# First layer in seven block products: batches 4 to 7 and all tails of a forgetting attention with a two-layer network, on one core

## The chip, the cores and the metric

The kernel runs on one core of one Trainium2 chip. The metric is the device time of one execution in microseconds (us); runs of the kernel before took 1084.06, 1081.60 and 1083.31, median 1083.31.

A core has five engines with instruction queues of their own, each worked through strictly in order: TensorE (PE, matmuls into eight PSUM banks), VectorE (DVE), ScalarE (ACT), GpSimd (POOL) and SyncE (SP), which here only issues DMA transfers.

## The reference

```python
# attention: B, H, S, D = 8, 8, 576, 64
scores = scale * np.matmul(q, k.transpose(0, 1, 3, 2))
cum = np.cumsum(np.log(np.clip(f, 0.0001, 1.0)), axis=-1)
decay = cum[:, :, :, None] - cum[:, :, None, :]
scores = np.where(causal, -1000000000.0, scores + decay)
attn = np.exp(scores - np.max(scores, axis=-1, keepdims=True))
attn = attn / (np.sum(attn, axis=-1, keepdims=True) + 1e-09)
attn_out = np.matmul(attn, v)
# network: 4608 tokens, 512 -> 2048 -> 512
x = attn_out.transpose(0, 2, 1, 3).reshape(B * S, H * D)
h = x @ w_in
g = np.maximum(h, 0.0) + alpha * np.minimum(h, 0.0)
out = g @ w_out
```

All inputs are 32-bit floats (the two weights come as 64-bit floats and are converted on the chip). To keep precision, a product of the network is made of three matmuls: each factor is split into a rounded part (hi) and the rest (lo), and hi x hi, hi x lo and lo x hi are added up in PSUM.

## The kernel before, in words

**Attention** goes over 32 head pairs n (8 batches of 4 pairs). For a pair, `load_n` fetches q, k and the decay rows and splits q and k into hi and lo (ScalarE copies, GpSimd subtracts; the first NN = 4 pairs use plain 32-bit matmuls instead and no split). `attention` then makes scores in stretches of TensorE, masks them and takes row minima on VectorE, takes exponentials on ScalarE, transposes on TensorE, evacuates on ScalarE, multiplies by v and divides by the sums, which go through a small DRAM tile `rd` to become rows. A batch has 576 tokens; the network takes the first 512 of each batch as one column group, and the last 64 of all eight batches together as a ninth group of 512, the *tails* (batch number 8 in the code, collected in the DRAM tile `xt`). `rest` divides, splits x into hi and lo and leaves it in the ring `rx` (seven buffers, four per batch).

**First layer**, `ffn1(b)`: for each of 16 blocks `fc` of 128 hidden features, 12 matmuls of 512 columns into one bank, in two halves of six; then ScalarE and VectorE apply the slopes and the result goes to the DRAM tile `hd`. For the groups in `LATE` = (0, 7, 8) the slopes are applied only later, in the second layer. The first weight is converted from 64 bits in `load_w_in`/`split64` (VectorE bit operations, ScalarE copies, GpSimd subtraction) during the early pairs.

**Second layer**, `ffn2(u)`, over 18 units of 256 tokens in the order `UNITS`: already in seven block products (the Strassen-Winograd scheme, `PRODS`): per unit 8 x 21 matmuls of 256 columns. Its factors are sums of blocks of h (VectorE), split on ScalarE and VectorE. The second weight is converted and its block sums are made in `load_w_out`, after attention, while the first layer of the last groups runs.

**Order.** Nothing is issued when it is written: `op(engine, ns, fn, key, deps, bufs)` records an operation with an estimated duration, and `Plan.run` is a list scheduler that writes the five queues: at each step the engine's operation that can start earliest, and among those the lowest key. Attention has keys of 10 per pair, the first layer 1e6 and more, so the first layer fills what attention leaves free on TensorE. `Ring` and `Store` hand out buffers in the order of their creation; an operation that needs a buffer waits until one is free. An operation marked `two=True` is planned to wait for GpSimd. At the end of attention `change` closes the pool of attention's buffers and opens those of the second layer (`o_change`, which depends on `done_a`).

Of the kernel before, what the change touches and what calls it, by code (L numbers as in the profile page):

```python
# [8 lines left out]
F32 = mybir.dt.float32  # L9
# [18 lines left out]
NV2 = 6  # L28
NS = 10
HURRY = 25  # L30
CONV0, CONV = 30, 2.2
NW = NF // 2
GW = 2
LATE = (0, B - 1, B)

UNITS = (2, 3, 0, 4, 5, 1, 6, 7, 14, 8, 9, 15, 10, 11, 16, 12, 17, 13)
# [42 lines left out]
SLACK = {"DVE": 1.12, "ACT": 1.08, "POOL": 1.05}  # L79
ENGS = ("PE", "ACT", "DVE", "POOL", "SP", "-")  # L80


class Plan:
# [30 lines left out]
    def run(self):  # L114
# [7 lines left out]
        while left:  # L122
            best = None
            for e in ENGS:
                t0 = self.now[e]
                pick = None
                for o in cand[e]:
# [17 lines left out]
                    if pick is None or (s, o.key) < pick[:2]:  # L145
                        pick = (s, o.key, o)
# [39 lines left out]
def attention_moe(  # L186
# [24 lines left out]
    xt = dram.tile([NP, 128, 512], F32, name="xt")  # L211
# [7 lines left out]
    am = const.tile([128, NF], F32, name="am")  # L219
# [14 lines left out]
    rH, rO = Ring(banks, 2, 4), Ring(banks, 0, 6)  # L234
# [9 lines left out]
    rrq = ring(sp, 2, [128, QW], F32, "rq")  # L244
    rrk = ring(sp, 2, [128, S], F32, "rk")
# [12 lines left out]
    rwa = ring(sp, 1, [128, 512], U32, "wa")  # L258
# [7 lines left out]
    wbf = sp.tile([128, 512], BF16, name="wbf")  # L266
# [29 lines left out]
    def split64(tiles, src, whi, wlo, key, deps, bufs_out):  # L296

        br, ba = Buf(rwr), Buf(rwa)
# [3 lines left out]
        a = lambda: shape(ba.t)  # L302
# [8 lines left out]
        def bits2():  # L311
# [7 lines left out]
                   key, [cp], [ba] + bufs_out) for h in (slice(0, 2), slice(2, 4))]  # L319
# [59 lines left out]
    o_wbf = op("DVE", 300, lambda: ve.memset(wbf, 1.0), -102)  # L379
    bw = Buf(rS)  # L380
    for i in range(7):
        op("PE", 800, lambda: [pe.matmul(bw.t, wbf[:, 0:128], wbf, start=True, stop=True) for _ in range(3)], -200, [o_wbf], [bw])  # L382
# [30 lines left out]
    x_ops, x_late, xt_ops, s_0 = {}, [], [], []  # L413

    def load_n(n, held):
# [4 lines left out]
        bq, bk, bZ = Buf(rrq), Buf(rrk), Buf(rZ)  # L420
        kq = -99 if first else -59 if n == 1 else kl
        dq = [] if first else [o_scan]
        l_q = op("SP", 450, lambda: sy.dma_start(bq.t, qq[b, p]), kq, dq, [bq], kb=320)
        l_k = op("SP", 450, lambda: sy.dma_start(bk.t, kk[b, p]), kq, dq, [bk], kb=288)
# [29 lines left out]
        rt = op("POOL", 260, lambda: po.tensor_tensor(Zt()[:, 512:576], Zt()[:, 512:576], tri2, ALU.add), kc + 0.3, tz + [o_mask], [bZ])  # L454
        if n < NN:
            held += [bq, bk]
            return [l_q, l_k], rz, rt, bZ, [(lambda: bq.t, lambda: bk.t)]
        bQ = Buf(rQ)
        Qh, Ql, Kh, Kl = ((lambda j=j: bQ.t[j]) for j in range(4))
        out = []  # L460
        for hi, lo, raw, ld, w in ((Qh, Ql, bq, l_q, QW), (Kh, Kl, bk, l_k, S)):
            o1 = op("ACT", c_acs(w), lambda hi=hi, raw=raw: ac.activation(hi(), raw.t, AF.Copy), kc, [ld], [raw, bQ])  # L462
            o2 = op("POOL", c_po(w), lambda hi=hi, lo=lo, raw=raw: po.tensor_tensor(lo(), raw.t, hi().bitcast(F32), ALU.subtract), kc, [o1], [raw, bQ])  # L463
            out += [o1, o2]
        held.append(bQ)
# [4 lines left out]
    def attention(n):  # L470
# [28 lines left out]
        def evac(bank, w, key, deps, dst, src, bufs):  # L499
            key -= hurry  # L500
            if b == 0 and w % 256 == 0:
                return op("DVE", c_dve(w), lambda: ve.tensor_copy(dst(), src()), key, deps, [bank] + bufs)  # L502
            return op("ACT", c_act(w), lambda: ac.activation(dst(), src(), AF.Copy), key, deps, [bank] + bufs)  # L503
# [78 lines left out]
        def fetch(key, st_, d):  # L582
            for o, (c0, c1), s0 in ((0, (0, S), 0), (64, (512, S), S), (64, (0, 512), S + 64)):
                ri_ops.append(op("SP", 350, lambda o=o, c0=c0, c1=c1, s0=s0: sy.dma_start(
                    bri.t[o : o + 64, c0:c1], d[s0 : s0 + c1 - c0].rearrange("(o s) -> o s", o=1).broadcast_to([64, c1 - c0])),
                    key, [st_], [bri], kb=(c1 - c0) / 4))

# [93 lines left out]
        def rest():  # L681
            bx, xo = Buf(rx), []
            for r in range(2):
# [3 lines left out]
                late = ri_ops if n < NN else [op("-", 2000, lambda: None, st, ri_ops)]  # L687
                mu = op("DVE", c_dve(w_), lambda r=r, t0=t0, w_=w_: ve.tensor_tensor(bxs[r].t, bxs[r].t, bri.t[:, t0 : t0 + w_], ALU.mult),  # L688
                        st, xs_ops[r] + late, [bxs[r], bri])
                xh = op("ACT", c_acs(256), lambda r=r, t0=t0: ac.activation(  # L690
                    bx.t[:, 0, t0 : t0 + 256], bxs[r].t[:, 0:256], AF.Copy), st, [mu], [bxs[r], bx])
                xl = op("POOL", c_po(256), lambda r=r, t0=t0: po.tensor_tensor(  # L692
                    bx.t[:, 1, t0 : t0 + 256], bxs[r].t[:, 0:256], bx.t[:, 0, t0 : t0 + 256].bitcast(F32), ALU.subtract), st, [xh], [bxs[r], bx])
                xo += [xh, xl]
                x_late.extend((mu, xh, xl))
            xt_ops.append(op("SP", 400, lambda: sy.dma_start(xt[p, :, 64 * b : 64 * b + 64], bxs[1].t[:, 256:320]), k0 + 11.6, [mu], [bxs[1]], kb=32))
            x_late.append(xt_ops[-1])
            x_ops[b, p] = [bx] + xo
# [13 lines left out]
        def values():  # L712
            bP = [Buf(rH if n < NP else rS) for _ in range(2)]
# [25 lines left out]
    w_ready = {}  # L739
    w_in_v = w_in.rearrange("(c p) f -> p c f", p=128)  # L740

    def load_w_in(fc):
        fs = slice(128 * fc, 128 * fc + 128)
        w_ready[fc] = split64(NC4, w_in_v[:, :, fs], lambda: wi[:, fc, 0], lambda: wi[:, fc, 1], CONV0 + CONV * fc, [s_0[6]], [])

    hd_ops, h_pe = {}, {}

    def ffn1(b):

        for fc in range(NF):  # L750
            bh, bs = Buf(rH), Buf(rhs)
            last = None
# [14 lines left out]
            else:  # L767
# [4 lines left out]
            hd_ops[b, fc] = op("SP", 400, lambda bs=bs, fc=fc: sy.dma_start(  # L772
                hd[fc % NW, fc // NW, :, 512 * b : 512 * b + 512], bs.t), -1000, [cp], [bs], kb=256)

# [6 lines left out]
    for fc in range(NF):  # L781
        load_w_in(fc)
    done_a = [o for o in plan.ops if o not in set(x_late)]

    TU = 256  # L790
    later = []

    def ring_later(n, shape, dt, name):
        r = Ring(Store([]))
        later.append((r, n, shape, dt, name))
        return r

    rwo = ring_later(2, [128, DM], U64, "wr2_")
    rwx = Ring(Store([]))
    rhr = ring_later(2, [128, GW, 2, TU], F32, "hr")  # L800
    rgx = ring_later(2, [128, 4, GW, 128], F32, "gx")
    rgh = ring_later(1, [128, 2, 7, GW, 128], F32R, "gh")
    ros = Ring(Store([]))
# [4 lines left out]
    wot = [None] * (NW - NV) + [wid[:, WN * i : WN * i + WN].rearrange("p (k j n) -> p k j n", k=2, j=7) for i in range(NV)]  # L808

    def change():  # L810
        ctx_a.close()
        p1 = ctx.enter_context(tc.tile_pool(name="p1", bufs=1, reuse_waits="tile"))
        for r, n, shape, dt, name in later:
            r.store.items += [p1.tile(shape, dt, name=f"{name}{i}") for i in range(n)]
            r.store.free += [(plan.t, i) for i in range(n)]
        wx.append(p1.tile([128, 2, 8, 256], F32, name="wx"))
        rwx.store.items += [wx[0][:, i] for i in range(2)]
        rwx.store.free += [(plan.t, i) for i in range(2)]
        for i in range(NW - NV):
            wot[i] = p1.tile([128, 2, 7, 256], F32R, name=f"wot{i}")  # L820
# [3 lines left out]
    def change3():  # L824
        st = rhr.store
        for i in range(4):
# [248 lines left out]
```

## Time and profile before

| | |
|---|---|
| median of the runs | 1083.31 us |
| the profiled execution | 1082.03 us |
| its span, first to last instruction | 1080.2 us |
| TensorE busy | 1068.2 us, 99% |
| VectorE, ScalarE, GpSimd busy | 707.3, 699.5, 279.4 us |
| granted TensorE clock, mean | 0.997 |
| HBM read and written | 120.68 and 48.52 MB |

A row of the timeline has the start in us, the length in us, engine, line, operation, output<-inputs (the program's names, buffer numbers left out), shape, and how many instructions were merged; in brackets the idle time before it and what ended it. A row of the groups has the total busy us and the mean ns of one. Matmuls overlap in a pipeline, so the length of a merged row divided by its count is nearer to what one costs than the mean. A row of the windows gives the stretch, its length, and for each engine the busy time and the number of instructions, then the granted clock, the share of the DMA engines and GB/s. Line L322 is the helper that issues most matmuls: `xx,wi` is the first layer, `wot` or `wi` with 256 columns the second, `Kh,Qh` the scores of a pair.

### The profile page before, as it was taken

Reading aid. Unit: us, or ns where it says so; the run is one execution under the profiler, and the core shown is the slowest. Engines: PE = TensorE matmul, PEld = TensorE weight load, DVE = VectorE, ACT = ScalarE, POOL = GpSimd, SP = SyncE. Lnnn points to the kernel's source line nnn. Section 1 sums busy time; section 2 is a strip of 40 time slices with the busy share of each in tenths; the row PEclk is TensorE's granted clock in tenths of the full one; section 3 lists DMA queues with packets and bytes.
Section 4 is the critical chain, followed back from the end, with each engine's and each line's share of the span. In section 5 each row is a group of like instructions: output and inputs, shape, how many; then the busy total and the mean of one; then the engine's idle time right before and its main releaser. Section 6 shows DMA issues by size and latency. Waiting matters only on the chain.

```text
span 1080.2 us, 20892 instructions
## 1 busy us (share of the span) xinstructions
PE 1068.2 (99%) x7428; PEld 910.8 (84%) x7428; DVE 707.3 (65%) x1632; ACT 699.5 (65%) x1638; POOL 279.4 (26%) x407
## 2 busy tenths in 40 slices
PE   8899999999999999999999999999999999999998
PEld 4577777777777777777787888899999999999998
DVE  6896745434434434434433497879989898989994
ACT  6898888967857857857846376656454554646551
POOL 6596774542443433433401000000000000000000
PEclk9999999999999999999999999999999999999999
DMA  6877766663653663553531566563433533443511
GB/s 184 252 221 239 241 193 180 191 182 115 184 174 118 179 181 115 177 177 115 151 104 71 166 221 233 193 206 117 150 126 118 157 118 120 139 134 125 147 61 39
DMA packets 116337, 170.57 MB, mean 158 GB/s; under 512 B 16626, under 2 KB 62601, under 8 KB 116233
## 3 DMA queue, kind: packets, MB, share of 16 engines
q1 hardware_dynamic: 115945, 169.05, 50.2%
q8 instruction: 58, 0.95, 0.4%
q14 instruction: 46, 0.38, 0.1%
q10 hardware_dynamic: 288, 0.20, 0.1%
HBM read 120.68 MB, written 48.52 MB: 157 GB/s over the span
## 4 chain that ended last, share of the span: by engine, by line
PE 96%; DVE 1%; DMA 1%; ACT 0%; POOL 0%; issue 0%; DVEq 0%
PE bank L322 87%; PE bank L507 8%; DMA wr<-in_w_in_dram 1%; PE bank L382 1%; DMA Zt<-c 0%; PE bank L646 0%; PE bank L571 0%; DVE xs L688 0%; ACT es L494 0%; DVE wa L313 0%; POOL Z L437 0%; DVE wa L312 0%; DVE e L527 0%; DVE eT L502 0%; DVE es L624 0%
## 5 line engine op out<-in xcount | busy, mean ns | idle before, releaser
L322 PE MATMUL bank<-xx,wi 128*128 128x512 f32 x1728 | 421.3, 396 | 0.3 <-DVE st L624 0.3
L322 PEld LDWEIGHTS bank<-xx,wi 128*128 128x128 f32 x1728 | 316.7, 188 | 63.3 <-issue 1.9
L770 DVE SCALAR_TENSOR_TENSOR hs<-bank,sa,hs 128x512 f32<-128x512 f32 x96 | 72.0, 750 | 156.6 <-ACT hs L768 156.6
L503 ACT ACTIVATE eT<-bank 128x384 f32<-128x384 f32 x240 | 109.2, 487 | 27.1 <-PE bank L507 23.7
L322 PE MATMUL bank<-wot,xx 128*128 128x256 f32 x1008 | 123.9, 284 | 0.0
L322 PE MATMUL bank<-wi,xx 128*128 128x256 f32 x1008 | 123.9, 284 | 0.0
L322 PEld LDWEIGHTS bank<-wi,xx 128*128 128x128 f32 x1008 | 122.3, 192 | 0.0
L322 PEld LDWEIGHTS bank<-wot,xx 128*128 128x128 f32 x1008 | 122.3, 192 | 0.0
L768 ACT ACTIVATE hs<-bank,ab 128x512 f32<-128x512 f32 x96 | 66.0, 687 | 81.0 <-PE bank L322 78.1
L494 ACT ACTIVATE e<-e,st 128x512 f32<-128x512 f32 (+2 forms) x160 | 109.1, 686 | 5.3 <-DVE st L527 3.4
L322 PE MATMUL bank<-eT,vr 128*64 128x320 f32 (+4 forms) x896 | 94.1, 360 | 0.0
L322 PEld LDWEIGHTS bank<-eT,vr 128*64 128x64 f32 x896 | 57.3, 137 | 40.8 <-issue 7.7
L507 PE MATMUL bank<-ident,e 128*128 128x128 f32 x576 | 87.9, 281 | 3.2 <-DVE st L624 1.6
L507 PEld LDWEIGHTS bank<-ident,e 128*128 128x128 f32 x576 | 68.2, 143 | 22.6 <-ACT e L494 6.0
L692 POOL TENSOR_TENSOR xx<-xs,xx 128x256 fp32r<-128x256 f32 x64 | 49.2, 785 | 146.7 <-ACT xx L690 146.7
L463 POOL TENSOR_TENSOR Ql<-rq,Qh 128x640 fp32r<-128x640 f32 x28 | 44.6, 1592 | 142.6 <-ACT Qh L462 57.8
L964 ACT ACTIVATE xx<-gx 128x1024 fp32r<-128x1024 f32 x48 | 50.8, 1058 | 30.8 <-PE bank L322 15.1
L437 POOL TENSOR_TENSOR Z<-Z,tri 128x384 f32<-128x384 f32 x64 | 61.9, 977 | 16.3 <-DMA Z<-c 8.8
L967 DVE TENSOR_TENSOR xx<-gx,xx 128x1024 fp32r<-128x1024 f32 x48 | 58.6, 1221 | 7.8 <-ACT xx L964 7.8
L322 PE MATMUL bank<-wi,gh 128*128 128x256 f32 x504 | 62.4, 284 | 0.0
L322 PE MATMUL bank<-wot,gh 128*128 128x256 f32 x504 | 62.4, 284 | 0.0
L322 PEld LDWEIGHTS bank<-wot,gh 128*128 128x128 f32 x504 | 61.4, 192 | 0.1
(137 smaller groups left out, 1690.0 us busy)
## 6 DMA issues: line engine op xcount, KB each, us to landing
hd<-hs SPq DMA_DIRECT2D x144, 256.0 KB, 2.0
wx<-hd SPq DMA_DIRECT2D x47, 512.0 KB, 4.1
Z<-c SPq DMA_DIRECT2D x62, 256.0 KB, 4.8
hr<-hd SPq DMA_DIRECT2D x25, 512.0 KB, 3.8
rq<-in_qq_dram SPq DMA_DIRECT2D x32, 320.0 KB, 5.3
vr<-in_vv_dram SPq DMA_DIRECT2D x32, 320.0 KB, 2.9
rk<-in_kk_dram SPq DMA_DIRECT2D x32, 288.0 KB, 3.4
Zt<-c SPq DMA_DIRECT2D x62, 144.0 KB, 5.0
```

The lines of the kernel that those rows point to most:

```text
L322: pe.matmul(o, lhsT, rhs, start=start, stop=stop)
L382: op("PE", 800, lambda: [pe.matmul(bw.t, wbf[:, 0:128], wbf, start=True, stop=True) for _ in range(3)], -200, [o_wbf], [bw])
L437: m1 = op("POOL", c_po(128 * 3), lambda z4=z4: po.tensor_tensor(z4()[:, 6:9], z4()[:, 0:3], tb(3), ALU.add), kc + 0.1, got + [o_mask], [bZ])
L463: o2 = op("POOL", c_po(w), lambda hi=hi, lo=lo, raw=raw: po.tensor_tensor(lo(), raw.t, hi().bitcast(F32), ALU.subtract), kc, [o1], [raw, bQ])
L494: ex = op("ACT", c_exp(w), lambda: ac.activation(bt.t[:, :w], bt.t[:, :w], AF.Exp, bias=lo()[:, col : col + 1], scale=-1.0, accum_out=su() ...
L503: return op("ACT", c_act(w), lambda: ac.activation(dst(), src(), AF.Copy), key, deps, [bank] + bufs)
L507: pe.transpose(t[:, c : c + 128], src[:, 128 * j : 128 * j + 128], ident)
L692: xl = op("POOL", c_po(256), lambda r=r, t0=t0: po.tensor_tensor(bx.t[:, 1, t0 : t0 + 256], bxs[r].t[:, 0:256], bx.t[:, 0, t0 : t0 + 256]. ...
L768: cp = op("ACT", c_act(512), lambda bh=bh, bs=bs, fc=fc: ac.activation(bs.t, bh.t, AF.Relu, scale=ab[:, fc : fc + 1]), -1000, [last, o_sg] ...
L770: cp = op("DVE", c_dve(512), lambda bh=bh, bs=bs, fc=fc: ve.scalar_tensor_tensor(bs.t, bh.t, sa[:, fc : fc + 1], bs.t, ALU.mult, ALU.add), ...
L964: his.append(op("ACT", c_acs(128 * GW * (j1 - j0)), lambda j0=j0, j1=j1, src=src, o_=o_: ac.activation(o_(0, j0, j1), src(), AF.Copy), key ...
L967: rdy.append(op("DVE", c_dve(128 * GW * (j1 - j0)), lambda j0=j0, j1=j1, src=src, o_=o_: ve.tensor_tensor(o_(1, j0, j1), src(), o_(0, j0, ...
```

## The change

1. **Groups of the first layer.** Batches 0 to 3 (`G = 4`) keep the plain `ffn1`. Batches 4 and 5, then the tails, then batches 6 and 7 are done by the new `strassen`: over eight pairs of feature blocks, seven products of six matmuls each (512 columns wide; 256 for the tails). `x_prep` loads x from DRAM, makes four sums and splits seven factors; each factor has one buffer. Results are added on VectorE, get their slopes on ScalarE, a last addition on GpSimd, and go to `hd`.
2. **Pace.** Block fc of batch b may begin only after the first scores of pair `int(PACE(b, fc))`, which rises from 6 to 31; blocks 6 to 15 of batch 3 wait for the last scores of all.
3. **x through DRAM.** Only batch 0 splits x where it is made. All others store it to `xd`; batches 1 to 3 are loaded back and split by `load_x` (ScalarE, GpSimd), 4 to 7 and the tails by `x_prep`.
4. **First weight.** `load_w_in` takes two blocks at a time in the one buffer of `rbx`, makes four block sums on GpSimd and stores them (`wsd`); after attention `load_ws` loads and splits them.
5. **Second weight.** `load_w_out` is spread over pairs 15 to 29 (key 150 + 20c), its block sums are made on GpSimd and stored (`wxd`); `load_wot` loads and splits them while the last group runs, into the space that this group gives up (`HOME`).
6. **Buffers and the planner.** Raw q and k: one buffer of `rraw` (the first pairs alternate with `rbx`) instead of two each. `LATE` is empty, `NV2` is 10 instead of 6, `UNITS` is in another order, products with v have a ring `rP` of their own, and of batch 0 only evacuations of 512 columns stay on VectorE. `Plan.run` sorts by key and, for GpSimd (`YIELD`), takes no operation that would keep one of a lower key waiting by more than 0.5 us.

```diff
-NV2 = 6
+NV2 = 10
-CONV0, CONV = 30, 2.2
+CONV0, CONV = 30, 3
+WO0, WO = 150, 20
+G = 4
+FK = 6
+TAILS = (B - G) // 2 - 1
+P0, P1 = 6, 31
+def PACE(b, fc):
+    return P0 + (P1 - P0) * (NF * b + fc) / (NF * G - NF + FK)
-LATE = (0, B - 1, B)
-UNITS = (2, 3, 0, 4, 5, 1, 6, 7, 14, 8, 9, 15, 10, 11, 16, 12, 17, 13)
+LATE = ()
+UNITS = tuple(range(14)) + (16, 14, 17, 15)
...
-    rrq = ring(sp, 2, [128, QW], F32, "rq")
-    rrk = ring(sp, 2, [128, S], F32, "rk")
-    rwa = ring(sp, 1, [128, 512], U32, "wa")
+    rraw = ring(sp, 1, [128, QW + S], F32, "raw")
+    rbx = ring(sp, 1, [128, 8, 256], F32, "bx")
...
+        def sums():
+            A11, A12, A21, A22, S1, S2, S3, S4 = (bx.t[:, i] for i in range(8))
+            po.tensor_tensor(S1, A21, A22, ALU.add)
+            po.tensor_tensor(S2, S1, A11, ALU.subtract)
+            po.tensor_tensor(S3, A11, A21, ALU.subtract)
+            po.tensor_tensor(S4, A12, S2, ALU.subtract)
+        su = op("POOL", 4 * c_po(256), sums, key + CONV, parts, [bx])
+        ws_ops[pr] = op("SP", 400, lambda: sy.dma_start(wsd[pr], bx.t[:, 4:8]), key + CONV, [su], [bx], kb=512)
...
         for fc in range(NF):
             bh, bs = Buf(rH), Buf(rhs)
-            last = None
+            late = b == G - 1 and fc >= FK
+            n = min(B * NP - 1, int(PACE(b, fc)))
+            last = s_0[-1] if late else s_0[3 * n if n < NE else 3 * NE + 2 * (n - NE)]
...
+    S_PRODS = (0, 1, 5, 4, 6, 2, 3)
+    def strassen(g, n, cols, units, xs_):
+        bX, ready = xs_
+        for pr in range(NW):
...
+            def product(m, dk, W=W):
+                jw, b_, bx = S_PRODS[m], Buf(rH), bX[m]
+                def f_():
+                    for c in range(2):
+                        for i, (k, l) in enumerate(((0, 0), (0, 1), (1, 0))):
+                            mm(b_.t[:, 0:n], W(jw, k, c), bx.t[:, l, c, 0:n], c + i == 0, c == 1 and i == 2)
...
+    o_x8 = op("-", 0, change2, 0, [o for q in xs_[1].values() for o in q])
+    op("-", 0, lambda: add(rgh, [as_gh(wide["xr"][:, 2048 : 2048 + WN])]), 0, [last[1], last[2]])
+    op("-", 0, change3, 0, list(last.values()) + res_ops[GL])
+    HOME = (4, 0, 5, 1, 6, 2, 7, 3)
```

417 lines of the change are left out of this document (283 added, 134 removed).

## The prediction

> **What bounds the kernel now.** I read the page's busy times first, then the chain that ended last, then TensorE's own row in time, stage by stage.
>
> ```profile
> PE 1068.2 (99%) x7428; PEld 910.8 (84%) x7428; DVE 707.3 (65%) x1632; ACT 699.5 (65%) x1638; POOL 279.4 (26%) x407
> PE 96%; DVE 1%; DMA 1%; ACT 0%; POOL 0%; issue 0%; DVEq 0%
> ```
>
> TensorE is busy 99% of the span and carries 96% of the chain, so time falls only with its work or its 12 us of idleness. What one matmul costs cannot be read from the mean durations, since neighbours overlap; it comes from long unbroken rows: start, length, count.
>
> ```profile
> 593.54 120.02 PE L322 MATMUL bank<-xx,wi 128*128 128x512 f32 x528
> 713.39 5.20 PE L322 MATMUL bank<-wot,gh 128*128 128x256 f32 x42
> 718.43 5.20 PE L322 MATMUL bank<-wot,xx 128*128 128x256 f32 x42
> 1066.18 10.24 PE L322 MATMUL bank<-wi,xx 128*128 128x256 f32 x84
> ```
>
> From 593.54 to 713.39 run 528 first-layer matmuls of 512 columns: 0.2270 us each. A second-layer run of 42 with 256 columns takes 718.43 - 713.39 = 5.04 us: 0.1200 each. The second layer goes from 713.39 to 1066.18 + 84 x 0.12 = 1076.3, that is 362.9 us without a gap, and 3.9 us of additions and stores end the span of 1080.2. Of the 1728 first-layer matmuls (9 batches x 16 blocks x 12), 1200 lie before 593.54, inside attention, where they fill what attention leaves free.
>
> ```profile
> 56.06 0.33 PE L322 MATMUL bank<-Kh,Qh 64*128 64x128 f32 x2
> 88.09 0.33 PE L322 MATMUL bank<-Kh,Qh 64*128 64x128 f32 x2
> 56.06:68.49 12.43, 1.66 (x6) 1.00 0.88 255
> 68.49:88.09 19.60, 10.98 (x42) 1.00 0.64 186
> 56.06:68.49 12.43, 11.39 (x92) 8.97 (x91) 12.24 (x36) 10.45 (x32) 10.74 (x12) 1.00 0.88 255
> ```
>
> The first two rows are the first scores of head pairs n=4 and n=6. The next two are windows with the first-layer matmuls alone (window, length, busy, count): 48 of them, 10.9 us, ran before pair 6. The last has all engines (TensorE, weight loads, VectorE, ScalarE, GpSimd): of 12.43 us of pair 4, TensorE was busy 11.39. From 88.09 to 593.54 are 505.5 us with 1152 first-layer matmuls (261.5 us); the other 244 us are the attention of 26 pairs, 9.4 us each.
>
> **The work that goes.** 1728 matmuls of 512 columns become 768 plain ones (batches 0 to 3), 2 x 8 x 7 x 6 = 672 in block products, and 336 of 256 columns for the tails: 288 x 0.2270 = 65.4 us go, 336 x 0.1200 = 40.3 come, net -25.1 us, all of it on TensorE and so on the path.
>
> **The paced stage.** The plain blocks now wait for attention: block k of 54 may start after the first scores of pair 6 + 25k/54, 2.16 blocks (5.9 us) per pair; the other ten wait for the last scores. If TensorE stays full a pair takes 9.4 + 5.9 = 15.3 us. The old kernel already has such pairs:
>
> ```profile
> 344.72:359.36 14.64, 14.64 (x109) 11.36 (x109) 6.41 (x24) 11.96 (x36) 6.31 (x9) 1.00 0.63 186
> 359.36:373.90 14.54, 14.54 (x108) 11.28 (x107) 8.09 (x25) 12.73 (x36) 8.06 (x11) 1.00 0.66 181
> 346.54 1.64 PE L322 MATMUL bank<-xx,wi 128*128 128x512 f32 x6
> 349.36 2.92 PE L322 MATMUL bank<-xx,wi 128*128 128x512 f32 x12
> 357.47 1.63 PE L322 MATMUL bank<-xx,wi 128*128 128x512 f32 x6
> ```
>
> Two whole pairs of 14.64 and 14.54 us with a full TensorE; the first holds 6 + 12 + 6 = 24 first-layer matmuls, two blocks. So 2.16 blocks are about what a pair can swallow, and the old surplus filling is not needed once pairs 8 and later run. Into pairs 15 to 29 comes the conversion of the second weight:
>
> ```profile
> L312 DVE SCALAR_TENSOR_TENSOR wa<-wr,wa 128x512 uint32<-128x512 uint32 x16 | 14.3, 897 | 0.5
> L882 DVE SCALAR_TENSOR_TENSOR wx<-wr,wx 128x512 uint32<-128x512 uint32 x16 | 11.1, 693 | 0.5
> L878 ACT ACTIVATE wx<-wr 128x512 f32<-128x512 f32 x16 | 10.6, 664 | 0.0
> L891 ACT ACTIVATE wx<-wx,sg 128x512 f32<-128x512 f32 x16 | 11.5, 719 | 3.2 <-DVE wx L886 3.2
> L692 POOL TENSOR_TENSOR xx<-xs,xx 128x256 fp32r<-128x256 f32 x64 | 49.2, 785 | 146.7 <-ACT xx L690 146.7
> L690 ACT ACTIVATE xx<-xs 128x256 fp32r<-128x256 f32 x64 | 24.6, 409 | 7.2 <-DVE xs L688 5.8 <-PE bank L322 1.3
> ```
>
> Sixteen halves over 14 pairs are 1.14 a pair: ScalarE 1.14 x (0.664 + 0.719) = 1.6 us, VectorE at most 1.14 x 4 x 0.9 = 4.1 us, GpSimd eight sets of four sums, 8 x 4 x 0.785 / 14 = 1.8 us. Out of pairs 4 and later go two ScalarE copies (0.8) and two GpSimd subtractions (1.6); batches 1 to 3 get them back as reloads, about a quarter. ScalarE thus stands at some 13 to 13.7 of 15.3 us, VectorE at 10 to 12. I take 1 us for all pairs together; the upper bound is the rival below. About 100 DMA issues are added to SyncE's in-order queue in attention (w_out loads, x stores and reloads, two kinds of weight stores) and some 46 stores of the first layer leave it; a store that waits for GpSimd's sums holds back the loads behind it, and those of q and k now have one raw buffer.
>
> Row and rule here: the same instruction took 897 ns in the first weight's conversion, beside a busy GpSimd, and 693 ns in the second's, beside an idle one. [...]
>
> **The start.** Pairs 4 and 5 now run with no filling, and the raw q and k of pair 4 need the single buffer that pair 3 holds until its last scores.
>
> ```profile
> 39.08 0.35 SPq L423 DMA_DIRECT2D rq<-in_qq_dram  x1
> 51.56 1.50 PE L322 MATMUL bank<-rk,rq 64*128 64x512 f32 x2 [2.62 <-DVE st L527]
> rq<-in_qq_dram SPq DMA_DIRECT2D x32, 320.0 KB, 5.3
> hd<-hs SPq DMA_DIRECT2D x144, 256.0 KB, 2.0
> L462 ACT ACTIVATE Qh<-rq 128x640 fp32r<-128x640 f32 x28 | 20.4, 730 | 0.0
> L463 POOL TENSOR_TENSOR Ql<-rq,Qh 128x640 fp32r<-128x640 f32 x28 | 44.6, 1592 | 142.6 <-ACT Qh L462 57.8 <-DMA Z<-c 42.3 <-issue 15.4
> L463 POOL TENSOR_TENSOR Kl<-rk,Kh 128x576 fp32r<-128x576 f32 x28 | 41.2, 1471 | 28.3 <-ACT Kh L462 27.2 <-issue 1.1
> ```
>
> The old load went out at 39.08. The new one goes at 53.1, when pair 3's last scores end; 5.3 to land, 0.7, 1.6 and 1.5 to split, and pair 4 begins at 62.3 instead of 56.06. Behind it pairs 4 and 5 take 11.1 (12.43 less its 1.36 of filling) to 12.4 us each; I take 11.8, so pair 6 begins at 86. Bounds: 82 (pair 3 without its 2.62 us wait, pairs of 11.1), 91 (two pairs of 14.3, with the first weight's conversion in them). The old kernel was at 88.09, but with 10.9 us of first layer done: a loss of 86 - (88.09 - 10.9) = 8.8 us (5 to 14).
>
> Then the first weight: one buffer holds two blocks from their first bits until their sums are stored, at least 2 x 4 x 0.8 on VectorE (between the 897 and 693 ns above), 4 x 0.785 on GpSimd and 2 to 4 for the store (256 KB land in 2.0 us), 12 to 14 us, against 14 us in which the pace uses them up. GpSimd was already busy 10.74 of 12.43 us above. I take 2 us of TensorE waiting for weights (0 to 7).
>
> **The handovers.** Ten blocks (27 us) cover the end of attention and the preparation of the first block products. One x buffer per product means that a new group's factor is split only after the old group's last use.
>
> ```profile
> L964 ACT ACTIVATE xx<-gx 128x1024 fp32r<-128x1024 f32 x48 | 50.8, 1058 | 30.8 <-PE bank L322 15.1 <-DVE gx L951 8.2 <-DVE xx L967 4.3
> L967 DVE TENSOR_TENSOR xx<-gx,xx 128x1024 fp32r<-128x1024 f32 x48 | 58.6, 1221 | 7.8 <-ACT xx L964 7.8
> L994 DVE TENSOR_TENSOR hs<-bank,hs 128x512 f32<-128x512 f32 x17 | 11.8, 692 | 17.6 <-ACT xx L964 11.9 <-PE bank L322 3.9 <-ACT gh L964 1.5
> L768 ACT ACTIVATE hs<-bank,ab 128x512 f32<-128x512 f32 x96 | 66.0, 687 | 81.0 <-PE bank L322 78.1 <-DMA ri<-rd 2.1
> 810.00:837.00 27.00, 27.00 (x228) 27.00 (x227) 24.30 (x45) 13.21 (x23) 0.00 (x0) 1.00 0.37 118
> ```
>
> Inside a group nothing is late: one pair of blocks gives TensorE 42 x 0.227 = 9.5 us, VectorE 7 x 0.69 = 4.8, ScalarE 9 x 0.69 = 6.2 at most, GpSimd four sums of 512, about 4 x 1.3 = 5.2 (by the 576-wide row). From the tails to batches 6 and 7, products shrink to 6 x 0.12 = 0.72 us: the first factor is split 4.3 us before the new group and ready after 1.06 + 1.22, in time; the others follow every 1.22 + 0.69 = 1.9 us while a product takes 1.36, so the seventh is at -2.0 + 6 x 1.9 = 9.4 against 8.2: 1.2 us late, some 3 where GpSimd interferes. Into the first group I take nothing (0 to 5; VectorE's 11 passes of 1.22 fit into 27 us if the four x loads land in half of it). At the second layer's start the second run's factor buffer comes free only when the last results are added, about 3.4 us after the last product, and its split takes 1.06 + 1.22 and two shorter ones, against 5.04 us: 1 to 2 us, on a VectorE that this stage fills to 24.30 of 27. The added copies of the old LATE units there go, which ends no wait. Together 4 us (1 to 12).
>
> **Sum.** From pair 6 on: 244 (attention) + 64 x 12 x 0.227 = 174.3 + 152.5 (672 products) + 40.3 + 362.9 + 3.9 = 977.9; with 86 before it and 2 + 1 + 4 of waits, 1070.8 against 1080.2 us of span, -9.4. The profiled execution took 1082.03, 1.3 under the median 1083.31; in terms of the median I forecast 1074.
>
> **Rivals.** *Nearly all of it stays*: pair 6 at 83, one wait in all, 1080.2 - 1062 = 18: 1065. For it: TensorE was full in the two pairs above, at nearly this load. Against: two pairs without any filling.
> *Attention becomes the bound* (slower): conversion steps stand in front of the exponentials on ScalarE and the masks on GpSimd, and TensorE has no surplus blocks to fill with. If pairs 15 to 29 go at 14.6 + 1.6 (ScalarE) + 0.4 (what is left of GpSimd's) = 16.6 us instead of 15.3, fourteen pairs lose 18: 1092. It decides from 16.0 us a pair on. [...]
> *The handovers and the start take it all*: upper bounds of 14 and 7 with 4 of handovers make up the 25.1 that goes: 1083, no change.
>
> **Chances.** Forecast 0.45; nearly all 0.19; no change 0.12; attention bound 0.24. Hence faster by over 0.2% (2.2 us, about what a measurement of this kernel can tell from no change) 0.64, within it 0.12, slower 0.24. Range 1062 to 1092: it leaves out the upper half of the attention rival and a little below the best case.
>
> **What would show it.** Right: 768 plain and 672 product matmuls of 512 columns, 336 of 256; pair 6 near 86 with a first idle stretch of TensorE before pair 4; pairs of 15 to 15.5 us afterwards; waits of 1 to 3 us where groups change. Wrong: pairs above 16 us with TensorE waiting for ScalarE or VectorE in many small steps, waits for wi before pair 13, or a gap of over 10 us where attention ends.

## The result, and the profile after

The changed kernel takes 1143.96 us (median of four runs, 1141.08 to 1145.55) beside 1082.77 for the kernel before: ratio 1.0562, 95% interval 1.0537 to 1.0587. The forecast was 1074, the range 1062 to 1092. The profiled execution took 1145.55 us, with a span of 1143.6.

The page of the changed kernel: busy times, TensorE's row and its granted clock in 40 slices, and the chain that ended last.

```profile
PE 1076.0 (94%) x7478; PEld 916.6 (80%) x7478; DVE 805.9 (70%) x1735; ACT 746.2 (65%) x1679; POOL 455.4 (40%) x539
...
PE   8887999999999998999699998998999999999998
...
PEclk9978999999999999999799999998999999999999
...
PE 74%; DVE 8%; ACT 6%; DMA 4%; POOL 4%; issue 3%; SPq 1%; POOLq 0%; DVEq 0%; ACTq 0%
```

TensorE has fallen from 99% busy and 96% of the chain to 94% and 74%. Its busy time has *risen* by 7.8 us (1068.2 to 1076.0) although 25.1 us of matmuls went. The third row gives most of the reason: the clock falls in several slices, and a matmul at a lower clock is busy for longer (28 value products take 5.60 us at clock 0.50 and 2.93 at 1.00, shown further down).

TensorE's waits (releaser: us in total, times, longest):

```profile
PE bank L529 <- ACT e L516: 23.0, 14, 3.3
PE bank L341 <- DVE wr L978: 6.7, 2, 5.0
PE bank L341 <- POOL Kl L486: 5.9, 4, 2.8
PE bank L341 <- ACT wr L976: 4.7, 1, 4.7
```

Before, this view had 8 us in all. Now 23.0 us are attention's transposes waiting for an exponential, and 6.7 + 4.7 = 11.4 us are waits for the block products' factors, nearly all of it two long ones. By stage (window, length, TensorE busy, clock, DMA share, GB/s), the groups beginning at 547.62 and the second layer at 767.40:

```profile
58.29:77.52 19.23, 16.57 (x82) 0.56 0.38 104
77.52:93.46 15.94, 11.61 (x92) 0.97 0.81 250
195.75:506.12 310.37, 293.48 (x2080) 0.98 0.75 240
547.62:638.55 90.93, 80.22 (x337) 0.92 0.42 149
```

The first two are pairs 4 and 5, the third pairs 12 to 30, the last the first group of block products.

**Where the 63.4 us of span come from.** TensorE not busy: 1143.6 - 1076.0 = 67.6 us against 12.0 before, +55.6. Work: -25.1. Lower clock: the means, 0.970 against 0.997, give 1143.6 x 0.030 - 1080.2 x 0.003 = +31, but part of the low clock falls on time in which TensorE waits, and the first term holds that time already. On busy time alone, by the rows below, it is 27.6 - 3.4 = +24.2. The sum is +54.7 of +63.4; the other 9 us are busy time that neither the count of matmuls nor the clock explains, and they stay open. The clock is not in the prediction at all.

The clock can be read stretch by stretch. These are windows of the changed kernel cut where the clock changes (window, length, busy, clock, DMA share, GB/s), all eleven stretches below full clock:

```profile
51.00:56.00 5.00, 3.40 (x15) 0.66 0.92 303
58.00:76.00 18.00, 15.84 (x79) 0.53 0.35 102
92.00:103.00 11.00, 8.23 (x39) 0.53 0.79 255
218.00:223.00 5.00, 5.00 (x26) 0.66 0.83 329
235.00:240.00 5.00, 5.00 (x31) 0.66 0.90 209
293.00:298.00 5.00, 4.07 (x19) 0.66 0.61 177
553.00:568.00 15.00, 7.81 (x19) 0.54 0.64 209
642.00:646.00 4.00, 3.92 (x18) 0.57 0.88 281
693.00:697.00 4.00, 4.00 (x12) 0.57 0.52 151
775.00:779.00 4.00, 4.00 (x20) 0.57 0.46 135
785.00:789.00 4.00, 3.84 (x20) 0.57 1.03 333
```

Length times what lacks to 1.00 gives 1.7, 8.5, 5.2, 1.7, 1.7, 1.7, 6.9, 1.7, 1.7, 1.7 and 1.7 us, 34 in all; with the busy time in place of the length it is 27.6. The short ones all lose 1.7 us, as much as 3.4 us at clock 0.50 would: the windows of 0.5 us from 693.0 to 697.0 show 0.90, six times 0.50, and 0.69. In all eleven stretches the lowest such window shows 0.50. The kernel before has two of these (18 to 22 and 52 to 56 us, 3.4 us by busy time), and none after 56.

### The profile page after: what moved, and what is told of

It is laid out like the page before. It is cut to its first block, busy times and chain, and to the rows that moved or that the text cites. A ratio compares the mean times of both kernels' runs of the same rounds, so it can differ in the third digit from the quotient of the medians.

```text
span 1143.6 us, 21755 instructions
## 1 busy us (share of the span) xinstructions
PE 1076.0 (94%) x7478; PEld 916.6 (80%) x7478; DVE 805.9 (70%) x1735; ACT 746.2 (65%) x1679; POOL 455.4 (40%) x539
## 4 chain that ended last, share of the span: by engine, by line
PE 74%; DVE 8%; ACT 6%; DMA 4%; POOL 4%; issue 3%; SPq 1%; POOLq 0%; DVEq 0%; ACTq 0%
PE bank L341 68%; PE bank L529 5%; ACT eT L525 1%; ACT e L516 1%; DMA Zt<-c 1%; POOL hs L1034 1%; DVE sr L1026 1%; DVE xs L713 1%; DVE wr L978 1%; ACT hs L865 1%; PE bank L401 1%; POOL Kl L486 1%; DMA ri<-rd 1%; DMA wr<-in_w_in_dram 1%; DVE hs L867 1%
## 5 line engine op out<-in xcount | busy, mean ns | idle before, releaser
L341 PE MATMUL bank<-xx,wi 128*128 128x512 f32 (+1 forms) x1056 | 262.3, 393 | 3.5 <-DVE xx L978 2.1
L341 PEld LDWEIGHTS bank<-xx,wi 128*128 128x128 f32 x1056 | 187.4, 190 | 42.9 <-DVE xx L978 2.9
L1034 POOL TENSOR_TENSOR hs<-sr,hs 128x512 f32<-128x512 f32 (+1 forms) x96 | 120.5, 1265 | 99.9 <-ACT sr L1033 97.8
L1026 DVE TENSOR_TENSOR sr<-bank,sr 128x512 f32<-128x512 f32 (+1 forms) x168 | 98.8, 600 | 66.1 <-PE bank L341 32.4
L341 PE MATMUL bank<-wr 128*128 128x256 f32 (+1 forms) x813 | 131.9, 316 | 13.3 <-DVE wr L978 6.7
L341 PEld LDWEIGHTS bank<-wr 128*128 128x128 f32 x813 | 116.2, 196 | 23.0 <-DVE wr L978 7.4
L525 ACT ACTIVATE eT<-bank 128x384 f32<-128x384 f32 (+1 forms) x248 | 109.9, 479 | 31.6 <-PE bank L529 27.3
L341 PE MATMUL bank<-wr,xx 128*128 128x256 f32 x987 | 127.3, 284 | 0.0
L341 PEld LDWEIGHTS bank<-wr,xx 128*128 128x128 f32 x987 | 122.8, 193 | 0.0
L1172 DVE TENSOR_TENSOR xx<-sr,xx 128x256 fp32r<-128x256 f32 x141 | 105.4, 784 | 18.3 <-ACT xx L1169 17.9
L1169 ACT ACTIVATE wr<-sr 128x256 fp32r<-128x256 f32 (+2 forms) x75 | 52.2, 702 | 55.6 <-PE bank L341 43.9
L1032 ACT ACTIVATE hs<-sr,ab 128x512 f32<-128x512 f32 (+1 forms) x96 | 61.5, 641 | 31.4 <-DVE sr L1026 21.9
```

The lines of the kernel that those rows point to most:

```text
L341: pe.matmul(o, lhsT, rhs, start=start, stop=stop)
L1026: return bd, op(eng, (c_dve if eng == "DVE" else c_po)(n), lambda: e.tensor_tensor(bd.t[:, 0:n], b_.t[:, 0:n], bc.t[:, 0:n], ALU.add), -10 ...
L1032: ac.activation(bh.t[:, 0:n], b_.t[:, 0:n], AF.Relu, scale=ab[:, fc : fc + 1]),
L1034: r_ = op("POOL", c_po(n), lambda: po.tensor_tensor(bh.t[:, 0:n], b_.t[:, 0:n], bh.t[:, 0:n], ALU.add), 1.05e6, [r_], [b_, bh])
L1169: his.append(op("ACT", c_acs(128 * GW * (j1 - j0)), lambda j0=j0, j1=j1, src=src, o_=o_: ac.activation(o_(0, j0, j1), src(), AF.Copy), key ...
L1172: rdy.append(op("DVE", c_dve(128 * GW * (j1 - j0)), lambda j0=j0, j1=j1, src=src, o_=o_: ve.tensor_tensor(o_(1, j0, j1), src(), o_(0, j0, ...
```

## The experiments

Theory A was the prediction's slower rival: the second weight's conversion makes attention the bound. Theory B: the pace leaves TensorE no block to run while attention waits for an exponential; the old surplus did that. Theory C: such waits and the unfilled start lower TensorE's clock. Smaller questions were the cover of the first block products and the price of the first weight's sums and of the single raw buffer. "Idle" is TensorE's waiting in a stage, "cold" a stretch below full clock.

**e1_noconv**, theory A, the conversion out (two loads of other data take its place):

```diff
 def load_w_out(c):
...
-            sq = op("ACT", c_acs(512), lambda hi=hi, sq_=sq_, s2=s2: ac.activation(sq_(), s2(hi()).bitcast(F32), AF.Square), key, [ld], [br, bx])
...
-        su = op("POOL", 4 * c_po(256), sums, key, done, [bx])
+        half = lambda j: bx.t[:, 4 * j : 4 * j + 4].rearrange("p k n -> p (k n)")
+        su = [op("SP", 400, lambda j=j: sy.dma_start(half(j).rearrange("p (h q) -> p h q", h=2), qq[c, 2 * j : 2 * j + 2, :, 0:512].rearrange("h p q -> p h q")), key, [s_0[6]], [bx], kb=512) for j in range(2)]
```

> The changed kernel with the second weight's conversion left out of attention: its buffer is filled from q by two DMA loads of the same size and stored as before, so the output is not the reference's. ScalarE's 32, VectorE's 64 and GpSimd's 32 instructions of it go. Theory A (conversion makes attention the bound): pairs 15 to 29 fall from 16.0 us on average to about 14.5, TensorE's waits for exponentials nearly vanish there, and the kernel takes 1115 to 1125. Theory B (attention has no surplus first-layer blocks left to fill its bubbles, and a TensorE that has waited then runs at a lower granted clock): pairs stay at 15.5 to 16 and the kernel takes 1135 to 1145.

Measured: 1149.05 us, ratio 1.0602 (1.0572 to 1.0633). The last pair starts at 511.8 us (changed kernel: 506.1), and TensorE still waits, in the waits view:

```profile
PE bank L529 <- ACT e L516: 20.1, 12, 3.8
```

Theory A falls: with all that work gone, the same waits for the same exponentials remain. The time is also above the 1135 to 1145 expected under theory B.

**e2_g6** and **e3_g8**, theory B: more plain blocks, fewer in products. The edit of e2; e3 has 8 in its place.

```diff
-G = 4
+G = 6
```

> The changed kernel with six plain batches (0 to 5) instead of four and one 512-wide product group instead of two: 10.9 us more TensorE work by count, 3.5 blocks a pair instead of 2.16 to fill with. Theory B: bubbles and cold stretches of attention shrink, its last pairs run with TensorE full; of the 33 us that attention lost against the forecast some 20 to 25 come back, and one handover of 6 goes: 1120 to 1130. Theory A: attention is slowed further by the added evacuations, 1155 or more.

> The changed kernel with all eight batches plain and only the tails in products: 21.8 us more TensorE work than the change, 4.7 blocks a pair. Theory B: attention as full as in the kernel before, two handovers fewer: 1105 to 1120, what is left over 1083 being the start and the one handover. Theory A: 1160 or more.

Measured: 1132.32 us, ratio 1.0448 (1.0418 to 1.0478), and 1126.50, 1.0394 (1.0358 to 1.0430), both faster than the changed kernel and both above their expected ranges. Pairs 12 to 30 of each, first G = 6, then G = 8:

```profile
204.00:550.00 346.00, 342.05 (x2309) 1.00 0.71 229
```

```profile
206.40:517.20 310.80, 308.29 (x2167) 1.00 0.72 223
```

With G = 4 TensorE was idle there for 310.37 - 293.48 = 16.9 us at clock 0.98; with a surplus it is idle 4.0 and 2.5 us at 1.00. G = 8 runs its pairs in 310.8 us, as long as G = 4, and has done more first layer by the end of them: the added blocks go into waits. Theory B holds for this stage. The two variants do more TensorE work than the changed kernel and are still 1 to 2% faster. But G = 8, with pairs 4 and 5 at clock 0.77 over 34 us, is still 43 us behind the kernel before: the start and other parts cost that.

**e4_warm**, theories B and C: small dummy matmuls in every pair from 4 on.

```diff
+    def keep_warm(n):
+        for r in range(6):
+            bd = Buf(rH)
+            op("PE", 3 * 250, lambda bd=bd: [pe.matmul(bd.t[:, 0:128], ident, ident, start=True, stop=True) for _ in range(3)],
+               3e6 + r, [s_0[-1], o_id], [bd])
...
+        if n >= NE:
+            keep_warm(n)
```

> The changed kernel with six short idle tasks per pair (three 128-wide matmuls of the identity each, result unused) that TensorE may take when nothing else is ready. Theory B in its clock part: the granted clock stays near 1.00 in attention, TensorE's work in pairs 4 to 6 no longer takes twice its time, and the kernel takes 1120 to 1130. If the low clock only accompanies the waits and does not lengthen anything: 1145 to 1155, the tasks' own time being added.

Measured: 1229.12 us, ratio 1.1341 (1.1308 to 1.1374). The design failed as a whole: the dummies took the banks' ring in order, so that every plain block came behind them, after attention. One stretch is still of use, pairs 12 to 30:

```profile
190.60:432.60 242.00, 240.78 (x2202) 1.00 0.70 210
```

Filled with small pieces instead of blocks (13.4 - 9.4 = 4 us a pair), TensorE is full and a pair takes 13.4 us (pairs 6 to 31), with the second weight's conversion among them. Attention itself therefore does not need 16.5 us a pair; it does without the blocks' additions on ScalarE and VectorE here, though, so this is a bound and not a price.

**e5_cover**, the first block products: all of batch 3 after attention (16 blocks as cover instead of 10).

```diff
-FK = 6
+FK = 0
```

> The changed kernel with sixteen blocks instead of ten behind the last scores (FK = 0). The x loads of the first product group went out 15 us before the plain blocks ended, since they wait until attention's memory is free, and two of their four sums stood behind an addition that waits for the second product. Theory H (too short a cover): 16 us more cover remove the first group's waits of 4.7 and 5.0 us and its low clock, the group takes 77 to 79 us instead of 91, and the kernel 1130 to 1137, less what six blocks fewer cost inside attention. If the order of the queue alone is to blame, the waits stay and the kernel takes 1143 to 1150.

Measured: 1150.03 us, ratio 1.0613 (1.0564 to 1.0663). The first group:

```profile
569.77:645.93 76.16, 76.16 (x338) 1.00 0.41 144
```

76.2 us with no gap, which is 336 x 0.227, against 90.9 us: the cover decides this handover. The total does not gain, because six blocks fewer are left for attention; waits between pairs 6 and 12 grow from 6.8 to 16.8 us. That is theory B again, from the other side. (The total lies where the other expectation had put it, but the waits of the first group are gone.)

**e6_warm456**, theory C: dummies in pairs 3 to 6, in a ring of their own.

```diff
+    rD = Ring(banks, 0, 1)
+    def keep_warm(n):
+        for r in range(8):
+            bd = Buf(rD)
+            op("PE", 2 * 230, lambda bd=bd: [pe.matmul(bd.t[:, 0:128], ident, ident, start=True, stop=True) for _ in range(2)],
+               3e6 + r, [s_0[-1], o_id], [bd])
...
+        if NE - 1 <= n < NE + 3:
+            keep_warm(n)
```

> The changed kernel with eight short idle tasks of TensorE (two 128-wide matmuls of the identity each, result unused, a bank ring of their own) for each of pairs 3 to 6, about 15 us of work in all that can stand only where nothing else is ready. Clock theory: the granted clock in pairs 4 and 5 rises from 0.75 towards 1.00, pair 6 begins at 86 to 90 instead of 93.5 and the kernel takes 1137 to 1142. If the low clock lengthens nothing: pair 6 at 94 or later, 1145 to 1155.

Measured: 1153.13 us, ratio 1.0642 (1.0591 to 1.0693); pair 6 at 97.5 us, clock 0.61 in pair 4. Most dummies landed behind the waits that they were meant to fill. One place is a test: 28 of them ran at 47.01, ahead of the transposes that wait 3.32 us in the changed kernel (51.90). Here these wait 0.46 us, and the clock of that stretch is 1.00 instead of 0.66:

```profile
50.86 0.98 PE L529 MATMUL bank<-ident,e 128*128 128x128 f32 x7 [0.46 <-ACT e L516]
51.00:56.00 5.00, 2.27 (x19) 1.00 0.96 348
```

That agrees with theory C at this place. The next wait (2.80 us at 56.07) was not filled, and pair 4 behind it is as cold as before. As a whole the kernel is slower; it does not show that a higher clock would pay.

**e7_nosum**, the first weight's sums:

```diff
-        su = op("POOL", 4 * c_po(256), sums, key + CONV, parts, [bx])
-        ws_ops[pr] = op("SP", 400, lambda: sy.dma_start(wsd[pr], bx.t[:, 4:8]), key + CONV, [su], [bx], kb=512)
+        ws_ops[pr] = op("-", 0, lambda: None, key + CONV, parts, [bx])
```

> The changed kernel without the first weight's block sums and their store in attention (32 GpSimd sums, 8 stores; the later load takes x instead, so the output is not the reference's). If the first weight's buffer and GpSimd delay the start: pair 6 begins at 86 to 90, pair 12 at 183 to 188 instead of 196, the kernel takes 1130 to 1137. If not: 1142 to 1147.

Measured: 1126.75 us, ratio 1.0399 (1.0346 to 1.0452): some 17 us less than the changed kernel, which I had priced at 2. Not at the start: pair 6 comes at 96.2 us, later than 93.5. The gain lies behind it: the waits between pairs 6 and 12 go from 6.8 to 2.9 us, those from pair 12 to 31 from 16.9 to 10.4, and the last pair starts 12.9 us earlier. From pair 6 to pair 31 this kernel takes 397.0 us and the changed one 412.7.

**e8_raw1**, the single raw buffer, in the kernel *before*:

```diff
-    rrq = ring(sp, 2, [128, QW], F32, "rq")
-    rrk = ring(sp, 2, [128, S], F32, "rk")
+    rrq = ring(sp, 1, [128, QW], F32, "rq")
+    rrk = ring(sp, 1, [128, S], F32, "rk")
```

> The kernel before with one buffer each for raw q and raw k instead of two. By the forecast's step (the load of pair 4 waits for pair 3's last scores) pair 4 begins at about 62 instead of 56 and the kernel takes 1086 to 1089. If the load is not what pair 4 waits for, or the surplus blocks hide it: 1082 to 1085.

Measured: 1094.98 us, ratio 1.0106 (1.0050 to 1.0161), some 11 us and more than either expectation. Pair 4 starts at 67.9 us instead of 56.1:

```profile
0.00:67.90 67.90, 53.58 (x298) 0.92 0.60 180
```

67.9 - 53.58 = 14.3 us without work before pair 4 (6.5 in the kernel before) and 0.08 x 67.9 = 5 us of lost clock (3.4); from there on TensorE is nearly full (1.3 us of waits). The end is late by about what the start was: a kernel whose TensorE is full later has nothing to give it back with.

But this is not the start of the changed kernel. There the first pairs alternate with `rbx`, so the q of pairs 1 to 3 is fetched at 2.48, 15.58 and 23.72 us, about as in the kernel before (2.48, 14.13, 24.34); here each load waits for the pair before it and goes out at 15.00, 31.42 and 45.87. The load for pair 4, in the changed kernel and in this one:

```profile
48.65 0.33 SPq L448 DMA_DIRECT2D raw<-in_qq_dram  x1
```

```profile
58.86 0.39 SPq L423 DMA_DIRECT2D rq<-in_qq_dram  x1
```

Pair 4 begins at 58.29 in the changed kernel, 2.2 us later than before, not 11.8. So these 11 us are no price of the change as it was made.

**e9_gate6**, the other half of the start, in the kernel before: only the barrier.

```diff
-            last = None
+            last = s_0[3 * NE + 2 * (6 - NE)]
```

> The kernel before with one part of the change alone: its first layer may not start before the first scores of pair 6 (its raw buffers, its surplus of blocks and everything else stay). Theory C (an unfilled stretch costs the clock): pairs 4 and 5 run with TensorE half idle, the granted clock from pair 4 to pair 6 falls from 1.00 to some 0.75, these two pairs take 30 us or more as they do in the changed kernel (35.2), and the kernel takes 1083 plus the 10.9 us of blocks that ran there minus 32 us plus that time: 1093 or more. Rival (pairs without filling take 11.1 to 12.4 us each, as I forecast): pair 6 near 80 instead of 88, total 1083 to 1087.

Measured: 1088.63 us, ratio 1.0048 (1.0033 to 1.0063). Pairs 4 and 5, and the 8 us behind them:

```profile
55.20:64.55 9.35, 8.82 (x77) 0.97 0.89 247
64.55:79.44 14.89, 11.82 (x88) 0.89 0.58 172
79.44:87.44 8.00, 7.72 (x40) 0.57 0.95 302
```

The two unfilled pairs take 24.2 us; I had forecast 2 x 11.8 = 23.6. Theory C's 30 us do not come, nor does its 1093; the rival's pair 6 near 80 is right, and its upper bound of 1087 is passed. The clock does fall in pair 5 and behind it (cold at 66 to 70 and 79 to 87, 5 us lost), which is about the whole 5 us that this kernel lost. The stretch at 66 follows no wait above 0.5 us in the 16 us before it:

```profile
64.55 0.32 PE L322 MATMUL bank<-Kh,Qh 64*128 64x128 f32 x1 [0.48 <-DVE st L624]
66.00:70.00 4.00, 4.00 (x24) 0.57 0.86 283
```

So a long wait is not the only thing that goes before a lower clock; what did it here was not tried. The barrier alone is cheap. In the changed kernel the same two pairs took 35.2 us, 11 more.

**e10_fill45**, theory C: dummies in TensorE's own order, ahead of the transposes and value products of pairs 4 and 5.

```diff
     def blocks(t, c, src, js):
+        for _ in range(6 if NE <= n < NE + 2 and c == 0 else 0):
+            pe.transpose(t[:, 0:128], ident, ident)
...
+                for _ in range(6 if NE <= n < NE + 2 else 0):
+                    pe.transpose(o[:, 0:128], ident, ident)
```

> The changed kernel with six identity transposes ahead of each transpose and of each value product of pairs 4 and 5, in TensorE's own order, so that they run while it waits for the exponentials: some 9 x 6 x 0.11 = 5.9 us of added work per pair. Theory C (the waits lower the clock, and the low clock is most of the loss there): the granted clock from 58 us to pair 6 rises from 0.75 to 0.93 or more, the 28 value products of pair 4 take about 3 us instead of 5.60, and pair 6 starts at 93 or earlier although 11.8 us of work were added. Rival (the other engines set the pace of these pairs, and the low clock only accompanies it): the value products are faster but pair 6 still starts at 93 to 96. Third possibility: the clock stays under 0.85 although TensorE waits less; then idle time is not what lowers it.

Measured: 1145.31 us, ratio 1.0569 (1.0542 to 1.0596). Two windows of it, pair 4 and the place of the second long cold stretch:

```profile
59.00:77.00 18.00, 16.19 (x90) 0.57 0.38 109
92.00:103.00 11.00, 10.11 (x84) 1.00 0.88 271
```

In pair 4 the dummies stand behind the stretch: a pair's value products run in the time of the next pair, so the 28 at 69.60 are pair 3's and got none. The first dummies are at 75.05 us, when the stretch is over, and this place is not tested. At 92 they do what theory C says: the wait there shrinks, in the timelines of the changed kernel and of this one,

```profile
91.44 1.14 PE L529 MATMUL bank<-ident,e 128*128 128x128 f32 x7 [2.52 <-ACT e L516]
```

```profile
94.00 0.66 PE L531 MATMUL bank<-ident,e 128*128 128x128 f32 x4 [0.68 <-ACT e L516]
```

and the clock stays at 1.00 from 92 to 103 where it had been 0.53. Pair 6 still starts later (96.7 us): the dummies cost more than they saved. "Waits lower the clock" is shown at this place and at the first wait of e6; that keeping it up pays is not.

**e11_g8_nosum**, do the parts add? The edit of e7_nosum, and

```diff
-G = 4
+G = 8
```

> G = 8 (no block products at all) and also without the GpSimd sums of the first weight and their store; without block products nothing reads those sums, so the output stays that of the reference. What is left of the change is the barred start, the single raw buffer, the pace and the second weight's conversion in attention. If the sums cost as much here as in the changed kernel (17 us): 1126.5 - 17 = 1109. Rival: with blocks in surplus to the end, TensorE hides them, and it gains 3 to 8 us only: 1119 to 1123.

One sentence of that was wrong: at G = 8 the tails still go in block products and read those sums, so this kernel leaves them out, as e7 does, and the tails get other data. Measured: 1115.06 us, ratio 1.0293 (1.0266 to 1.0320), 11 us less than G = 8. That is between the two expectations: a surplus of blocks hides part of the sums' 17 us, not most of it.

**e12_p05**, one pair less of barrier:

```diff
-P0, P1 = 6, 31
+P0, P1 = 5, 31
```

> The changed kernel with P0 = 5: the first layer may start one pair earlier, and the pace stretches from pair 5 to 31. Theory C: pair 5 gets filling, so the clock recovers one pair earlier; pair 6 starts at 92 to 96 with some 5 us of blocks done, later pairs get 2.08 blocks instead of 2.16: total 1138 to 1144, a gain of 0 to 6 us. Rival (weights are late so that the early blocks wait and hold up attention, and sparser blocks make more bubbles later): 1144 to 1150.

Measured: 1143.54 us, ratio 1.0550 (1.0521 to 1.0579): no difference from the changed kernel that can be told. Both mechanisms show, with opposite signs:

```profile
92.00:103.00 11.00, 9.37 (x70) 0.84 0.75 221
198.20:511.40 313.20, 291.32 (x2050) 0.97 0.75 236
```

The clock after pair 6 recovers earlier (0.84 instead of 0.53), and the waits of pairs 12 to 30 grow from 16.9 to 21.9 us, since the blocks are spread thinner.

## Why the prediction was wrong, point by point

**Work: right.** The groups by line count 960 + 192 + 192 + 96 = 1440 first-layer matmuls of 512 columns, the 768 + 672 forecast. e5's first group of 76.16 us is 336 x 0.2267.

**The paced stage: wrong, and with the handovers the largest miss.** The failed step is "If TensorE stays full a pair takes 9.4 + 5.9 = 15.3 us", with "2.16 blocks are about what a pair can swallow, and the old surplus filling is not needed". From pair 6 (93.46) to the end of the plain blocks (547.62) went 454.2 us; full, it is 244 + 174.3 = 418.3. Of the 35.9 beyond, 6.8 + 16.9 + 0.8 = 24.5 are waits, and the cold stretches from 93 to 298 lengthen what runs in them by about 8.7; 2.7 stay open. My two old pairs of 14.6 us were full because the planner could take a block *whenever* a wait came. With a pace, a pair has 24 or 36 block matmuls and no more, and where they are used early the later wait is bare. Pair 17 (280.96 to 299.70), all its blocks and the wait behind them:

```profile
282.37 1.66 PE L341 MATMUL bank<-xx,wi 128*128 128x512 f32 x6
284.22 1.64 PE L341 MATMUL bank<-xx,wi 128*128 128x512 f32 x6
287.12 1.66 PE L341 MATMUL bank<-xx,wi 128*128 128x512 f32 x6
288.86 1.63 PE L341 MATMUL bank<-xx,wi 128*128 128x512 f32 x6
...
293.93 0.84 PE L529 MATMUL bank<-ident,e 128*128 128x128 f32 x3 [2.24 <-ACT e L516]
294.70 0.79 PE L341 MATMUL bank<-Kh,Qh 64*128 64x512 f32 x2
```

No block is left at 291.7; TensorE waits 2.24 us, and the last row shows the second price: two matmuls take 0.79 us at clock 0.50, and the same two take 0.50 us at 1.00 (83.12 us). e2 and e3 add blocks and the waits go; e5 and e12 thin them and the waits grow. This is shown by four runs. The pace is not alone in it: without the first weight's sums (e7) pairs 6 to 31 take 15.7 us less at the same pace, so a part of the same 35.9 us goes with either.

**The slower rival.** Its sign and its sign to look for (pairs above 16 us, here 16.5, with many waits for ScalarE) came true, its mechanism did not: e1 takes the conversion out and gains nothing. Why ScalarE's exponentials come later than the plan has them is open.

**The start.** Pair 6 came at 93.46, not at 86, outside my bound of 91. Up to pair 4 the mechanism held: its load went out at 48.65, when pair 3's last scores ended, and pair 4 began 9.6 us later, at 58.29 (forecast: 53.1, 9.2 us later, 62.3). The failed step is "pairs 4 and 5 take 11.1 (...) to 12.4 us each; I take 11.8": they took 19.23 and 15.94. e9 shows that the barrier alone gives 24.2 us for both, as forecast; the other 11 come from something else in the change, and e8's loss, which lies ahead of pair 4, is not it. Pair 4's 18 us cold are about 7.4 us of them (15.84 us busy at clock 0.53): 28 value products take 5.60 us there and 2.93 in pair 5:

```profile
69.60 5.60 PE L341 MATMUL bank<-eT,vr 128*64 128x320 f32 x28 [1.57 <-DVE st L648]
...
84.25 2.93 PE L341 MATMUL bank<-eT,vr 128*64 128x320 f32 x28 [0.17 <-ACT eT L525]
```

Why pair 4 stays cold for 18 us although TensorE is busy in 15.84 of them is not settled: the dummies of e6 and e10 did not reach it.

**The first weight's waits: 2 us forecast (0 to 7), 17 in e7** (11 in e11). I priced matmuls that wait for `wi`. TensorE waits for exponentials, the split keys and the statistics instead. That GpSimd's added sums delay the splits on the same queue fits the 5.9 us of waits for `Kl`, and VectorE's slower passes (893, 897 and 844 ns before in the first weight's conversion, 969, 900 and 919 now) may add to it; which one carries the rest was not tried.

**VectorE beside GpSimd.** The sum has no term for slower passes of VectorE. The second weight's conversion does get slower where it now stands: its four passes took 421, 693, 689 and 693 ns before, while GpSimd was busy in 1.6 of 86 us (617 to 703), and take 532, 771, 828 and 1178 ns now, while it is busy in 139.2 of 249 us (226 to 475). Whether GpSimd is what lengthens them was not tried by itself. As e1 gains nothing without these passes, leaving them off the path was right.

**The handovers: 4 us forecast (1 to 12), 36 measured.** The first group, the tails and the second group took 767.40 - 547.62 = 219.8 us instead of 152.5 + 40.3 = 192.8, the second layer 376.2 instead of 366.8. Of these 36.4 us, 18.1 + 4.9 = 23.0 are waits, the five cold stretches from 553 on lengthen what runs in them by 10.4, and 3 stay open. The failed step is "Ten blocks (27 us) cover the end of attention and the preparation of the first block products", with "Into the first group I take nothing": that group took 90.9 us instead of 76.2. The x loads wait for attention's memory; they were issued at 532.75, 15 us before the products, and the queue of VectorE has an in-order trap:

```profile
544.31 2.47 DVE L969 TENSOR_TENSOR sr<-sr 128x1024 f32<-128x1024 f32 x2
550.61 0.69 DVE L1026 TENSOR_TENSOR sr<-bank,sr 128x512 f32<-128x512 f32 x1 [3.83 <-PE bank L341]
...
552.63 2.48 DVE L969 TENSOR_TENSOR sr<-sr 128x1024 f32<-128x1024 f32 x2
555.03 2.30 DVE L978 TENSOR_TENSOR wr<-sr,wr 128x1024 fp32r<-128x1024 f32 x1
```

The addition at 550.61 belongs to the second product and waits for TensorE; the next two sums stand behind it, though their data are there, and so TensorE waits for what VectorE could have made meanwhile (and after them a division of attention's last x, 2.02 us at 557.25, stands ahead of the next split):

```profile
547.62 2.88 PE L341 MATMUL bank<-wr,wi 128*128 128x512 f32 x12
555.24 0.79 PE L341 MATMUL bank<-wr 128*128 128x512 f32 x1 [4.74 <-ACT wr L976]
560.98 5.06 PE L341 MATMUL bank<-wr 128*128 128x512 f32 x11 [4.95 <-DVE wr L978]
```

Two waits of 9.7 us and a low clock behind them (11 matmuls in 5.06 us at clock 0.50; 12 take 2.88 at 547.62, at 1.00). e5's longer cover removes all of it. The later handovers' waits are each about as long as forecast, 1 to 3 us (1.76 at 642, 1.68 and 1.82 at 689 and 692, 2.03 and 1.79 at 775 and 784), but there are five of them, 9.1 us where I had 4 in all, and four were followed by 1.7 us of lost clock each.

**What stays open.** G = 8 without the sums is still 32 us behind the kernel before, with 3 us less TensorE work. Its idle time (1112.0 - 1080.4 = 31.6 us, 19.6 more than before) and its clock (0.983; some 12 us more by busy time) account for 31 of these 35. e9's barrier, 5 us, is a part of it; e8's 11 us are not, since pair 4 begins at 56.65 here. How much the pace, the planner's new order and the tails' handovers carry of the rest was not separated. No variant here is faster than the kernel before.

## What to carry to other kernels

Work that can run at any time is worth more than its own duration: before pacing or removing it, count the waits that it fills now, and give each a place. Where TensorE carries the time, price a wait of 2 us at its length plus the clock that it may cost behind it (here 1.7 to 8.5 us a stretch), and read the clock in windows of a few us; add up a lower clock over busy time only, since waiting time is counted already. For the cover of a handover, take the time from when its first load may be issued, and look on each in-order queue for an instruction that waits for the very engine that it feeds.

## What the runs showed of the hardware

I had not expected how short the waits are (1.76 us at 642) behind which TensorE's clock is lower. In the changed kernel 14 waits of 1.76 us or more stand in TensorE's timeline; 13 of them have a cold stretch behind or around them, and where dummies shortened the wait at 51.90 (e6, from 3.32 to 0.46 us) and the one at 91.44 (e10, from 2.52 to 0.68) the cold stretch was gone (clock 1.00 instead of 0.66 and 0.53). The exception:

```profile
455.53 0.55 PE L529 MATMUL bank<-ident,e 128*128 128x128 f32 x3 [2.60 <-ACT e L516]
```

Waits of 1.62, 1.56, 1.61 and 1.61 us (at 19, 329, 346 and 472 us) had none, but in the kernel before the one of 1.62 us at 17.35 had, and e9 has a cold stretch at 66 us behind a wait of 0.48. So the length of a wait alone does not decide. Each short stretch lost 1.7 us, and the long ones 5.2, 6.9 and 8.5, about three to five times that.
